# Attention scores with 128 query columns per matmul instead of 64, and values summed in five parts instead of four

## The chip, the cores and the metric

The kernel runs on one core of a Trainium2 chip. The metric is the device time of one execution in microseconds, lower is better. The engines of the core work side by side, each on its own instruction stream: TensorE (PE in the profile; its weight loads are listed apart as PEld), VectorE (DVE), ScalarE (ACT), GpSimd (POOL), and SyncE (SP), whose queue issues nearly all DMA transfers here.

## The reference

Two things follow each other: attention with a bias that depends on relative position, for 8 batches, 8 heads, 576 positions and a head size of 64, and a product of matmuls over all 4608 tokens.

```python
scores = scale * np.matmul(q, k.transpose(0, 1, 3, 2))
pos = np.arange(S)
rel = (pos[:, None] - pos[None, :]).astype(np.float32)
psi_rel = np.log1p(np.abs(rel))
psi_i = np.log1p(np.maximum(pos[:, None].astype(np.float32), 1.0))
x = (psi_rel / psi_i)[..., None]
h = np.maximum(x @ w1 + b1, 0.0)
bias = h @ w2
scores = scores + bias.transpose(2, 0, 1)[None, :, :, :]
scores = scores - np.max(scores, axis=-1, keepdims=True)
attn = np.exp(scores)
attn = attn / (np.sum(attn, axis=-1, keepdims=True) + 1e-09)
return np.matmul(attn, v).astype(np.float32)

a = x @ w1            # x: 4608 x 512, the attention's output
b = x @ w2            # w1, w2: 512 x 1024
h = a * b @ w3        # 1024 x 1024
return (h @ w_out).astype(np.float32)   # 1024 x 512
```

All is float32.

## The kernel before

**Stages.** A prologue (about 52 us) computes the bias table and writes it to DRAM (`bias_group`). Then come 32 attention *units*, one for each pair of heads and batch. Then the weights w3 and w_out are folded into one matrix (`fold`), and the expert stage runs over 9 chunks of 512 tokens (`up`, `down`).

**A unit.** A unit has 2 heads x 576 queries = 1152 query rows, cut into nine score tiles of 128 rows: tiles 0, 2, 4, 6 are the first 512 queries of one head, 1, 3, 5, 7 those of the other, and M holds the last 64 of both. The 576 keys are split in two halves of 288. The key half lies on partitions 0 to 63 or 64 to 127 (head size 64 each), and the queries lie there twice, so both halves of the array's rows can work at once. The steps of a tile t of unit u are:

- `S` (`op_S`, line 254, TensorE): the scores of the tile into a PSUM buffer `s` with two banks, one for each half of the keys. There are two such buffers.
- `T` (`op_T`, line 269, VectorE): scale, add the bias and take the extreme of each row in one instruction, from PSUM into SBUF. It frees the buffer `s`.
- `E` (`op_E`, line 293, ScalarE): the exponential, with the row sums.
- `R` (`op_R`, line 311, VectorE): a transpose in 32 x 32 blocks, for two tiles at a time (M alone), into `PT[u % 2]`.
- `W` (`op_W`, line 348, TensorE): the matmuls of the transposed probabilities with the values into `acc`, over 18 blocks of 32 keys. A unit's 18 blocks are cut by `PARTS` into parts W0, W1, ..., each of which has its own tile of values (`v0`, `v1`, ...; one buffer each), loaded by `lv0`, `lv1`, ... on SP. Each block takes 8 matmuls with 32 rows and 64 columns.
- `X` (`op_X`, ScalarE) copies `acc` to SBUF, and `xd` stores it. There is a single `acc`, so the next unit's W0 waits for X. `r` and `rd` handle the row sums of four units.
- `c0` to `c6` prepare a piece of the expert weights in units that have one (`c0` loads 512 KB).
- `lk`, `lq` load keys and queries.

**Order.** The order on each engine is written out by hand. `rhythm` (line 43) gives each step a time within a period of 12.17 us, and `arrange` shifts it by the unit's number; all steps are then sorted by time and issued, and every engine works strictly in that order. W and its loads lie one period after the scores of the same unit. In the steady state TensorE has this order within a period (the scores of unit u, W0 to W2 of unit u-1, W3 of unit u-2):

```
S0 S2 | W3 | S4 S6 | W0 | SM S1 | W1 | S3 S5 | W2 | S7 (next: S0 S2 ...)
```

VectorE's order is `T0 T2 R57 T4 T6 R02 TM T1 R46 T3 T5 [c5] RM T7 R13`, where R57 and R13 are those of the unit before or of this one, as they come due. With two buffers, S4 needs T0 done, S6 needs T2, SM needs T4, S1 needs T6, S3 needs TM, S5 needs T1, S7 needs T3, S0 of the next unit needs T5, and S2 needs T7.

One float32 matmul of the program appears in the trace as two MATMUL and two LDWEIGHTS records.

Of the kernel before, what the change touches and what calls it, by code (L numbers as in the profile page):

```python
# [18 lines left out]
P = 128  # L19
# [12 lines left out]
FIRST = "02134657M"  # L32
PAIRS = ("02", "46", "M", "13", "57")
NPP, NTS = 2, 3
PARTS = ((0, 5), (5, 9), (9, 12), (12, 18))
T_AT = 0.0, 0.66, 2.63, 3.29, 5.26, 5.92, 7.89, 8.55, 9.91
R_AT = 3.95, 6.58, 9.21, 10.57, PERIOD + 1.32
E_AT = 0.75, 2.75, 3.70, 4.65, 6.25, 7.20, 8.80, 9.75, 10.70
S_AT = -2.32, -1.52, 1.40, 2.00, 4.30, 4.90, 6.90, 7.50, 9.20
W_AT = 2.65, 5.55, 8.15, 11.35  # L40


def rhythm(tiles, turns):

    at = {}
    for n, t in enumerate(tiles):
        at["S" + t] = S_AT[n], "PE"
        at["T" + t] = T_AT[n], "DVE"
# [4 lines left out]
    at["rd"] = PERIOD + 3.80, "SP"  # L53
    for n, w in enumerate(W_AT):
        at[f"W{n}"] = PERIOD + w, "PE"
# [28 lines left out]
def relpos_attention_moe(  # L84
# [25 lines left out]
    HS = S // 2  # L110
# [94 lines left out]
    lo, hi = slice(0, 64), slice(64, 128)  # L205
# [33 lines left out]
    def op_l(u, which):  # L239
        p, b = units[u]  # L240
        n = int(which[1])
        if which[0] == "v":
            b0, b1 = PARTS[n]
            t = vp.tile([P, b1 - b0, 2, D], F32, name=f"v{n}")
# [9 lines left out]
    def op_S(u, t):  # L254

        d = st[u]
        s = d["s", t] = ps_s.tile([P, 2, 512], F32, name="s")
        for hf, rows in enumerate((lo, hi)):
            for g, outs in enumerate((lo, hi)):
                if t == "M":  # L260
                    h, q0 = g, 512
                else:
                    h, q0 = int(t) % 2, int(t) // 2 * P + 64 * g
                nc.tensor.matmul(  # L264
                    s[outs, hf, :HS], d[f"q{h}"][rows, q0:q0 + 64],
                    d[f"k{h}"][rows, :], start=True, stop=True,
                )

# [17 lines left out]
    for i in range(2):  # L286
        t = att.enter_context(tc.tile_pool(name=f"sums{i}", bufs=1)).tile([P, 64], F32, name=f"sums{i}")
# [60 lines left out]
    def op_W(u, n):  # L348
# [4 lines left out]
        acc, pt_ = d["acc"], PT[u % 2]  # L353
        for b in range(*PARTS[int(n)]):
            for a in range(4):
# [37 lines left out]
    def op_c(u, n):  # L393
        pieces[u][int(n)]()

    made = dict(l=op_l, S=op_S, T=op_T, E=op_E, R=op_R, r=op_r, W=op_W, X=op_X, x=op_x, c=op_c)
    later = []
    for (n, u), (at, on) in arrange(NU, pieces).items():
# [14 lines left out]
    with ExitStack() as pro:  # L413
# [29 lines left out]
        def reach(G):  # L443

            return (G + 1) * GR - 1, S - 1 - G * GR
# [9 lines left out]
        for G in range(NGRP):  # L455
            n = max(reach(G)) + 1
# [296 lines left out]
```

## Time and profile before

| | us |
|---|---|
| median of three timed runs | 1150.75 (1145.63 to 1157.9) |
| the profiled execution | 1149.57 |
| its span, first to last instruction | 1147.8 |
| mean granted TensorE clock | 0.985 |

| engine | busy us | share of the span |
|---|---|---|
| TensorE matmuls (PE) | 1070.3 | 93% |
| TensorE weight loads (PEld) | 781.9 | 68% |
| VectorE (DVE) | 638.4 | 56% |
| ScalarE (ACT) | 510.5 | 44% |
| GpSimd (POOL) | 180.2 | 16% |

The page cuts the span into 40 slices of 28.7 us and gives a digit of busy tenths for each. The granted clock is the share of its full speed that TensorE was allowed. Groups of instructions are named by line, engine, operation and tile (`out<-in`), with count, busy time, mean duration, and the idle time before them with what ended it ("issue": nothing that the profile shows). Matmuls are pipelined and the ends that the trace gives them are modelled, so from one burst of matmuls to the next it is the distance of starts that counts.

### The profile page before, as it was taken

What the parts mean: (1) busy time and instruction counts of PE and PEld (TensorE: products, weight loads), DVE (VectorE), ACT (ScalarE), POOL (GpSimd) and SP (SyncE); (2) the same over time, 40 slices, a digit from 0 to 9 for tenths busy, and PEclk for the clock granted to TensorE, in tenths of its full rate; (3) what the DMA queues carried; (4) which work ended last, traced back from release to release, by engine and by line L of the source; (5) the groups of instructions that cost most, each with busy time, mean ns of one, the idle gap of its engine ahead of it and who ended that gap; (6) DMA issues with size and microseconds to landing.
All of it is one profiled execution on the core that took longest, in us unless ns stands there. A gap on an engine that the chain in (4) does not pass through costs nothing.

```text
span 1147.8 us, 34051 instructions
## 1 busy us (share of the span) xinstructions
PE 1070.3 (93%) x14720; PEld 781.9 (68%) x14720; DVE 638.4 (56%) x1204; ACT 510.5 (44%) x1111; POOL 180.2 (16%) x167
## 2 busy tenths in 40 slices
PE   7888888888888999898999999999999999999998
PEld 2245555555555655576888888888888888888887
DVE  8997989889988999956551313222231322223111
ACT  7876767676766778765442111111212112121212
POOL 0022312230323033254350000000000000000000
PEclk9988999999989999999999999999999999999999
DMA  8966757767777667456240202111121202110000
GB/s 275 319 194 217 253 178 256 243 197 225 240 245 227 214 209 244 140 167 174 83 120 37 58 16 76 35 58 53 40 70 37 56 19 74 37 37 1 37 1 37
DMA packets 95957, 149.16 MB, mean 130 GB/s; under 512 B 22336, under 2 KB 49088, under 8 KB 95808
## 3 DMA queue, kind: packets, MB, share of 16 engines
q1 hardware_dynamic: 95376, 146.98, 40.4%
q8 instruction: 115, 1.88, 0.7%
q14 instruction: 34, 0.28, 0.1%
q10 hardware_dynamic: 432, 0.02, 0.0%
HBM read 116.93 MB, written 30.03 MB: 128 GB/s over the span
## 4 chain that ended last, share of the span: by engine, by line
PE 72%; DVE 13%; issue 8%; ACT 3%; DMA 2%; POOL 1%; SPq 1%; DVEq 0%; ACTq 0%; POOLq 0%
PE up L623 34%; PE o L648 17%; PE acc L360 9%; PE s L264 7%; DVE ts L275 6%; DVE pt L314 5%; PE bacc L485 3%; ACT x L369 1%; PE wacc L582 1%; DMA x_d<-x 1%; DMA v<-in_v_dram 0%; DVE wmag L159 0%; DMA rb<-r_m 0%; DVE mx L275 0%; ACT x L374 0%
## 5 line engine op out<-in xcount | busy, mean ns | idle before, releaser
L304 ACT ACTIVATE pp<-ts,mx 128x576 f32<-128x576 f32 x256 | 197.1, 770 | 103.4 <-DVE mx L275 102.4
L631 DVE TENSOR_TENSOR g<-up,a 128x512 f32<-128x512 f32 x72 | 49.8, 691 | 343.7 <-PE up L623 343.7
L360 PE MATMUL acc<-pt,v 32*64 32x128 f32 (+1 forms) x9216 | 208.1, 299 | 34.2 <-issue 27.9
L360 PEld LDWEIGHTS acc<-pt,v 32*64 32x64 f32 x9216 | 163.9, 133 | 99.2 <-issue 72.8
L623 PE MATMUL up<-xh,wl 128*128 128x512 f32 x576 | 225.1, 391 | 0.0
L623 PE MATMUL up<-xl,wh 128*128 128x512 f32 x576 | 225.1, 391 | 0.0
L623 PE MATMUL up<-xh,wh 128*128 128x512 f32 x576 | 225.1, 391 | 0.0
L264 PE MATMUL s<-k,q 64*64 64x288 f32 x2304 | 190.1, 434 | 25.0 <-DVE mx L275 24.2
L275 DVE CUSTOM_DVE_ANT_0 ts<-s,nb 128x576 f32<-128x576 f32 x256 | 183.4, 741 | 38.2 <-PE s L264 38.1
L648 PE MATMUL o<-w3s,gh 128*128 128x512 f32 x576 | 177.7, 390 | 0.0
L314 DVE STREAM_TRANSPOSE pt<-pp 128x1152 f32<-128x1152 f32 x128 | 175.9, 1375 | 0.0
L628 ACT COPY a<-up 128x512 f32<-128x512 f32 x72 | 42.2, 587 | 263.0 <-PE up L623 263.0
L264 PEld LDWEIGHTS s<-k,q 64*64 64x64 f32 x2304 | 74.5, 136 | 104.2 <-DVE mx L275 64.1
L623 PEld LDWEIGHTS up<-xl,wh 128*128 128x128 f32 x576 | 108.2, 188 | 23.4
L623 PEld LDWEIGHTS up<-xh,wl 128*128 128x128 f32 x576 | 108.2, 188 | 23.4
L623 PEld LDWEIGHTS up<-xh,wh 128*128 128x128 f32 x576 | 108.2, 188 | 23.4
L648 PEld LDWEIGHTS o<-w3s,gh 128*128 128x128 f32 x576 | 108.1, 188 | 22.9
L634 ACT ACTIVATE gh<-g 128x512 fp32r<-128x512 f32 x72 | 45.5, 632 | 173.7 <-DVE g L631 173.7
L648 PE MATMUL o<-w3s,gl 128*128 128x512 f32 x288 | 112.1, 389 | 0.0
L609 POOL TENSOR_SCALAR xh<-xr 128x512 fp32r<-128x512 f32 x36 | 22.6, 627 | 447.0 <-DVE xr L605 446.0
L155 POOL TENSOR_SCALAR wmag<-wmag 128x512 f32<-128x512 f32 x24 | 46.0, 1917 | 245.8 <-ACT wmag L145 245.8
L637 DVE TENSOR_TENSOR gl<-g,gh 128x512 fp32r<-128x512 f32 x72 | 50.8, 705 | 51.3 <-ACT gh L634 51.2
(68 smaller groups left out, 902.8 us busy)
## 6 DMA issues: line engine op xcount, KB each, us to landing
q<-in_q_dram SPq DMA_DIRECT2D x64, 288.0 KB, 4.0
wi<-in_moe_w_dram SPq DMA_DIRECT2D x32, 512.0 KB, 4.7
v<-in_v_dram SPq DMA_DIRECT2D x32, 384.0 KB, 5.4
nb_d<-bev SPq DMA_DIRECT2D x36, 295.5 KB, 4.7
v<-in_v_dram SPq DMA_DIRECT2D x32, 320.0 KB, 4.1
k<-in_k_dram SPq DMA_DIRECT2D x64, 144.0 KB, 3.4
nb<-nb_d SPq DMA_DIRECT2D x16, 576.0 KB, 5.8
x_d<-x SPq DMA_DIRECT2D x32, 288.0 KB, 4.8
```

What stands on the lines that cost most here:

```text
L155: clamps.tensor_scalar(d["mag"], d["mag"], LEAST, MOST, op0=ALU.max, op1=ALU.min)
L264: nc.tensor.matmul(s[outs, hf, :HS], d[f"q{h}"][rows, q0:q0 + 64], d[f"k{h}"][rows, :], start=True, stop=True,)
L275: nc.vector.tensor_tensor_reduce(out=halves(ts), in0=d.pop(("s", t))[:, :, :HS], in1=halves(NB[p, t]), op0=ALU.add, op1=ALU.min, scale=-1. ...
L304: nc.scalar.activation(d["p", ps][:, k * S:(k + 1) * S], ts, AF.Exp, bias=mx, scale=-1.0, accum_out=SUMS[u // 4 % 2][:, col:col + 1],)
L314: nc.vector.transpose(o, st[u].pop(("p", ts)))
L360: nc.tensor.matmul(acc[outs, a, c0:c0 + 32 * (t1 - t0)], d["v", b][rows, h], pt_[rows, t0:t1, 32 * b:32 * b + 32], start=(b == 0), stop=(b ...
L623: nc.tensor.matmul(acc, l[:, cc], r, start=(n == 0), stop=(n == 3 * NC - 1))
L628: nc.scalar.copy(a, ps[0])
L631: nc.vector.tensor_tensor(g, ps[1], a, op=ALU.mult)
L634: nc.scalar.activation(gh, g, AF.Copy)
L637: nc.vector.tensor_tensor(gl, g, f(gh), op=ALU.subtract)
L648: nc.tensor.matmul(d["o", t], l[:, sl], folded[ft][:, r], start=(ft == 0 and n == 0), stop=(ft == NF - 1 and n == 2),)
```

## The change

Tiles 0 to 7 of the scores are computed by two matmuls (one per half of the keys) that take all 128 queries as columns, instead of four that take 64 each. Tile M, whose two halves belong to different heads, keeps its four. The 18 blocks of values are cut into five parts (4, 4, 3, 4 and 3 blocks) instead of four (5, 4, 3 and 6), each with its own tile of values and its own load, and the times of the score and value steps in the period are moved. On TensorE the order becomes

```
S0 | W3 | S2 | W4 | S4 S6 | W0 | SM S1 | W1 | S3 S5 | W2 | S7 (next: S0 ...)
```

with W3 and W4 those of unit u-2. VectorE's and ScalarE's orders stay as they are. On SP there is one more load of values in a unit, `lv4`.

```diff
-PARTS = ((0, 5), (5, 9), (9, 12), (12, 18))
+PARTS = ((0, 4), (4, 8), (8, 11), (11, 15), (15, 18))
...
-S_AT = -2.32, -1.52, 1.40, 2.00, 4.30, 4.90, 6.90, 7.50, 9.20
-W_AT = 2.65, 5.55, 8.15, 11.35
+S_AT = -2.40, -0.55, 1.40, 2.00, 4.30, 4.90, 6.90, 7.50, 9.00
+W_AT = 2.65, 5.55, 7.95, 10.20, 12.25
...
         for hf, rows in enumerate((lo, hi)):
-            for g, outs in enumerate((lo, hi)):
-                if t == "M":
-                    h, q0 = g, 512
-                else:
-                    h, q0 = int(t) % 2, int(t) // 2 * P + 64 * g
+            if t == "M":
+                parts = [(outs, g, 512, 64) for g, outs in enumerate((lo, hi))]
+            else:
+                parts = [(slice(0, P), int(t) % 2, int(t) // 2 * P, P)]
+            for outs, h, q0, n in parts:
                 nc.tensor.matmul(
-                    s[outs, hf, :HS], d[f"q{h}"][rows, q0:q0 + 64],
+                    s[outs, hf, :HS], d[f"q{h}"][rows, q0:q0 + n],
                     d[f"k{h}"][rows, :], start=True, stop=True,
                 )
```

## The prediction

> **What bounds the kernel now.** I read the page first, then busy time by stretches, then the waits, then the order of one clean unit of work and of one disturbed one.
>
> ```profile
> span 1147.8 us, 34051 instructions
> PE 1070.3 (93%) x14720; PEld 781.9 (68%) x14720; DVE 638.4 (56%) x1204; ACT 510.5 (44%) x1111; POOL 180.2 (16%) x167
> DVE  8997989889988999956551313222231322223111
> q8 instruction: 115, 1.88, 0.7%
> PE 72%; DVE 13%; issue 8%; ACT 3%; DMA 2%; POOL 1%; SPq 1%; DVEq 0%; ACTq 0%; POOLq 0%
> ```
>
> VectorE is dense for the first 17 slices of 28.7 us (attention) and thin after them (the expert matmuls, where TensorE is dense). The change touches attention alone. The profiled execution took 1149.57 us, 1.8 us more than its span and 1.2 us under the median of the three timed runs (1150.75 us); I work against 1149.6.
>
> Two stretches follow: all of attention, and one unit (a head pair of one batch) inside it.
>
> ```profile
> 288.60:300.80 12.20, 11.08 (x378) 7.06 (x364) 12.20 (x25) 9.74 (x24) 3.19 (x2) 1.00 0.69 212
> 52.00:486.00 434.00, 376.36 (x11215) 232.90 (x11211) 394.47 (x780) 306.73 (x738) 108.23 (x87) 0.96 0.69 220
> ```
>
> After the length come PE, PEld, DVE, ACT, POOL with instruction counts, then granted clock, DMA share and GB/s. In the clean unit VectorE never rests (12.20 of 12.20), and TensorE has 1.12 us free. So VectorE sets the pace, nothing in the change shortens its work, and only its idle time can be won: 434.00 - 394.47 = 39.5 us in the whole of attention. The waits say for whom:
>
> ```profile
> PEld s L264 <- DVE mx L275: 64.1, 113, 2.0
> DVE ts L275 <- PE s L264: 40.7, 36, 4.1
> PE acc L360 <- issue: 27.9, 18, 3.3
> PEld acc L360 <- ACT x L374: 18.2, 29, 0.7
> ```
>
> Line 2: VectorE waits 40.7 us, 36 times, for score tiles. Line 3: TensorE, in the middle of the value matmuls, stands still 18 times for nothing that a semaphore shows, 27.9 us. One such case, TensorE, VectorE and the DMA engines around it:
>
> ```profile
> 197.14 0.79 PE L360 MATMUL acc<-pt,v 32*64 32x160 f32 x30
> 201.06 0.70 PE L360 MATMUL acc<-pt,v 32*64 32x160 f32 x18 [3.14 <-issue]
> ...
> 204.57 2.59 PE L360 MATMUL acc<-pt,v 32*64 32x160 f32 x96
> ...
> 202.58 0.76 DVE L275 CUSTOM_DVE_ANT_0 ts<-s,nb 128x576 f32<-128x576 f32 x1 [2.99 <-PE s L264]
> ...
> 196.00:198.00 2.00, 1.92 (x51) 1.00 (x47) 2.00 (x4) 1.57 (x6) 0.94 (x1) 1.00 0.97 338
> 198.00:200.00 2.00, 0.00 (x0) 0.00 (x0) 1.59 (x4) 1.56 (x4) 0.94 (x1) 1.00 1.05 395
> 204.00:206.00 2.00, 2.00 (x59) 1.43 (x55) 2.00 (x6) 1.42 (x4) 1.05 (x1) 0.50 0.73 207
> ```
>
> After 30 of 48 matmuls of W2 TensorE pauses 3.14 us; the DMA engines are full (0.97, 1.05) just then; VectorE pays 2.99 us; and the clock granted afterwards is 0.50, so that 96 matmuls take 2.59 us. The page's queue of instructions carried 115 packets, 1.88 MB: 16.3 KB each, and 2 x 14720 / 115 = 256 TensorE instructions each. I read these pauses as **instruction blocks that come late through busy DMA engines**. This is inferred from the coincidence, not shown.
>
> **The order in a clean unit**, from which the changed order is priced (start, modelled duration, idle before):
>
> ```profile
> 287.49 0.72 PE L264 MATMUL s<-k,q 64*64 64x288 f32 x8 [0.63 <-DVE mx L275]
> 288.13 1.91 PE L360 MATMUL acc<-pt,v 32*64 32x160 f32 x96
> 289.97 1.20 PE L264 MATMUL s<-k,q 64*64 64x288 f32 x16
> 291.35 1.67 PE L360 MATMUL acc<-pt,v 32*64 32x160 f32 x80 [0.18 <-ACT x L374]
> 292.94 1.20 PE L264 MATMUL s<-k,q 64*64 64x288 f32 x16
> 294.07 1.37 PE L360 MATMUL acc<-pt,v 32*64 32x160 f32 x64
> 295.37 1.20 PE L264 MATMUL s<-k,q 64*64 64x288 f32 x16
> 296.50 1.09 PE L360 MATMUL acc<-pt,v 32*64 32x160 f32 x48
> 297.53 1.20 PE L264 MATMUL s<-k,q 64*64 64x288 f32 x16
> 299.67 0.72 PE L264 MATMUL s<-k,q 64*64 64x288 f32 x8 [0.95 <-DVE mx L275]
> ...
> 288.64 0.72 DVE L275 CUSTOM_DVE_ANT_0 ts<-s,nb 128x576 f32<-128x576 f32 x1
> 291.27 0.72 DVE L275 CUSTOM_DVE_ANT_0 ts<-s,nb 128x576 f32<-128x576 f32 x1
> 293.89 0.72 DVE L275 CUSTOM_DVE_ANT_0 ts<-s,nbM 128x576 f32<-128x576 f32 x1
> 300.83 0.72 DVE L275 CUSTOM_DVE_ANT_0 ts<-s,nb 128x576 f32<-128x576 f32 x1
> ```
>
> A burst of two score tiles (16 records) lasts 1.13 us from its start to the next start (292.94 to 294.07), a lone tile 0.64 (287.49 to 288.13): a tile streams in 0.49 us, and a burst adds 0.15. Value matmuls: 96 in 1.84 us, 48 in 1.03 (296.50 to 297.53): 16.9 ns each and 0.22 per burst. One more burst of each kind in a unit therefore costs 0.37 us of TensorE.
>
> **The change, part by part.**
>
> *Two wide score matmuls for four narrow ones.*
>
> ```profile
> L264 PE MATMUL s<-k,q x2304: 399/403/739, 51.3 to 484.3; 64*64 64x288 f32 x192
> L264 PEld LDWEIGHTS s<-k,q x2304: 129/133/228, 51.3 to 484.0; 64*64 64x64 f32 x192
> L623 PEld LDWEIGHTS up<-xh,wh 128*128 128x128 f32 x576 | 108.2, 188 | 23.4
> ```
>
> Eight records of 403 ns fit into 0.49 us, so now the two halves of the keys and the two halves of the queries run side by side. With 128 query columns two matmuls lie side by side and stream the same 288 keys: I take 0.49 us again. No row shows this form. From below nothing can be gained in streaming, since the same keys pass; from above, if the two did not overlap, a tile costs 0.98. A weight load of 128 columns takes 188 ns (the expert matmuls' row) against 133: **+55 ns**. Inside a burst it hides behind the previous pass (0.24 us, half a tile); at the start of each of five bursts it doesn't: +0.27 us a unit. Records of L264 fall from 2304 to 2 x 32 x (8 x 2 + 4) = 1280 of each kind (M keeps four matmuls a tile), so attention issues 2 x 11213 - 2048 = 20378 TensorE instructions where it issued 22426: **9% less, 8 blocks of 256 fewer**.
>
> *Five value parts of 4, 4, 3, 4, 3 key blocks for 5, 4, 3, 6.* The order on TensorE goes from `S7 S0 S2 | W3 | S4 S6 | W0 | ...` to `S7 S0 | W3 | S2 | W4 | S4 S6 | W0 | ...`: matmuls in all unchanged, one score burst and one value burst more, +0.37 us a unit. Since M keeps its narrow form, the array also changes form between SM and S1; I price this as one more burst's fixed part, +0.15. In the clean unit S2 waits behind T7 with 0.95 us of idle, and W3 queues behind it. Now 64 value matmuls (1.30 us) run in that hole: S0 ends near 298.7, W3 near 300.0, S2 near 300.7; its reader T2 follows T0 (300.83 + 0.72), so S2 has 0.8 us to spare. W4 (48, 1.03 us) ends near 301.75; S4's buffer is free when T0 is done (301.55). Before, W3 ended at 302.16 on the same scale. So S4 comes 0.4 us sooner, against 0.05 for its wider load. W0 still waits for X (line 291.35), but with 64 matmuls ends 0.27 us sooner. The tightest place now is SM: it starts at 292.94, is done 0.64 later at 293.58, and TM starts at 293.89, **0.31 us of slack**; it becomes 0.31 + 0.27 = **0.58** (SM itself stays narrow; S1 behind it ended at 294.07, is due when TM is done, 294.61, and gains 0.27 less 0.15 and 0.05).
>
> *TensorE's account.* +0.37 + 0.27 + 0.15 = +0.79 us a unit, covered by the 1.12 us of idle; 0.33 is left. Without cover it would cost 32 x 0.79 = 25 us.
>
> *Loads.* The v parts change size with the blocks, bytes alike; 32 more issues on SP's queue. SP holds 1% of the chain; lv3 is issued when W3 has read its tile, ahead of c0 and xd, and W3 now ends sooner, so I cost it at nothing. If W3 were late, c0, xd and rd would queue behind that wait, but their readers come microseconds later. X follows W4 instead of the long W3, and ScalarE takes it behind E0 either way: nothing. The sums at the end (last units, expert stage) keep their work: nothing, within 1 us.
>
> **The Trainium skill** (Runtime: NRT & Kernel Launch, Instruction fetch mechanics) also says that instructions come in 16 KiB blocks of 256 while the previous block runs, and that crossing a boundary is "mostly hidden". The 16.3 KB per packet agrees; the 3.14 us pause does not look hidden. By that sentence fewer instructions win nothing, and the sum would be that of the second rival below.
>
> **The sum.** 18 pauses cost VectorE 40.7 us, 2.26 each (the 27.9 is only the part in which the array's modelled matmuls had ended). 9% fewer blocks: 1.6 fewer pauses, -3.7 us. The 16.4 that stay: a unit has (9 x 4 + 18 x 8) x 2 x 2 = 720 TensorE instructions and will have 656, so a block of 256 lasted 12.2 x 256 / 720 = 4.34 us and will last 4.76. A late block is late by up to 0.42 us less (0 if it is asked for only just before it is needed); I take 0.33, since most of a block's time, not all, should lie between request and need. Slack at the tightest place adds 0.27 (0 if a pause falls elsewhere); I take 0.22. 16.4 x 0.55 = -9.0 us. Together -12.7: 1149.6 - 12.7 = **1136.9**, say 1137; with both at nothing it is 1146, with both in full 1134.6.
>
> **Rivals.**
>
> 1. *The pauses belong to the transfers* (no difference). For: DMA share 0.97 and 1.05 at the pause shown; a block that is microseconds late because of 0.5 MB loads is not helped by 0.33. Against: most pauses are shorter than 3.3 us (27.9 / 18 = 1.55), where 0.55 is a third. Then only the 8 blocks count: -3.7, 1146. The three runs before already differ by 12 us, as chance arrival would make them.
>
> 2. *Nothing is hidden and nothing won* (slower): TensorE takes the lead from VectorE. Mechanism: the array changes from full-width score tiles to quarter-height value tiles eleven times a unit (SM to S1 counted) instead of eight. It decides from +1.12 us a unit; I count +0.79, so 0.03 us more per change is enough, and from there each 0.1 us per change costs 32 x 1.1 = 35 us. Taking the whole 0.79 uncovered: 1149.6 + 25 = 1175. For: SM's slack and the wait for X leave small holes, not one large one. Against: 0.33 is left, and 0.15 per score burst already holds both changes. The Trainium skill (TensorEngine Tiling, Key Properties) says that changing the tiling mode drains TensorE; the 0.15 and 0.22 agree, and no row here shows it for full width.
>
> 3. *The pauses nearly vanish*: if the missing lead is what turns late blocks into pauses, lead and slack take three quarters: 1149.6 - 30 = 1119. For: 18 pauses in 88 blocks, so the others just arrive. Against: the 3.14 us case.
>
> 4. *Wide matmuls don't overlap* (the change doesn't do what it says): 8 x 0.49 = 3.9 us a unit; TensorE 11.08 + 0.79 + 3.9 = 15.8 against 12.2; 32 x 3.6 = +115, 1265.
>
> **How the numbers follow.** Forecast 0.50 (own range 1127 to 1144), first rival 0.24, second 0.13, third 0.10, fourth 0.03. The range leaves out the fourth, the upper half of the second and the lowest part of the third: 1117 to 1162. One per cent, about what a measurement of this kernel can tell from no change, is 11.5 us. Under 1138 to 1139 lie 0.8 of the forecast and the third, 0.50; same has the rest of the forecast and the first, 0.34; slower the second and fourth, 0.16.
>
> **What would show it.** Score records 1280, a tile still 0.49 us apart in a burst (0.98: rival 4). First pass after a switch longer by about 55 ns. VectorE's wait for scores down from 40.7 to some 28 us, pauses in the value matmuls 16 or fewer; unchanged pauses mean rival 1. S2's idle before it gone from the clean unit, and a clean unit still 12.2 us; if VectorE waits in units without a pause, rival 2 is right. Wrong altogether would be a VectorE instruction that grew, or an expert stage that moved by more than 2 us.

## The result and the profile after

The changed kernel takes 1145.23 us (median of 21 runs, 1135.57 to 1148.85), the kernel before 1154.62 us in its 21 runs (1144.84 to 1163.95). The ratio is **0.9922, with a 95% interval of 0.9898 to 0.9946**: 9 us less, under one per cent. The forecast was 12.7 us less. A single run of either kernel scatters over 13 to 19 us, so differences of medians under some 4 us say little below. Sets of runs taken at different times differ too: the same changed kernel stands at 0.9879 and at 0.9839 [0.9799, 0.9879] of the kernel before in the two later sets. Kernels are therefore compared with those measured beside them.

The profiled execution took 1142.65 us. Its page, the parts that answer to those of before (length and counts; the instruction queue; TensorE's score matmuls by shape, from the groups with shapes kept apart):

```profile
span 1140.9 us, 32065 instructions
PE 1086.7 (95%) x13696; PEld 801.6 (70%) x13696; DVE 637.3 (56%) x1204; ACT 510.2 (45%) x1111; POOL 179.9 (16%) x167
q8 instruction: 107, 1.75, 0.6%
L264 PE MATMUL s<-k,q 64*128 64x288 f32 x1024 | 178.3, 453 | 9.0 <-DVE mx L275 3.7 <-DVE pt L314 2.5 <-issue 1.9
L264 PEld LDWEIGHTS s<-k,q 64*128 64x128 f32 x1024 | 86.6, 192 | 71.4 <-DVE mx L275 31.4 <-issue 27.2 <-DVE pt L314 3.7
```

TensorE has 2 x 1024 instructions less, and 8 packets fewer came over the instruction queue (107 for 115): 2 x 13696 / 107 is 256 again. The waits of attention, as before from 52 to 486 us (total, times, longest):

```profile
PEld s L264 <- DVE mx L275: 35.6, 106, 2.3
DVE ts L275 <- PE s L264: 28.0, 27, 2.5
PEld acc L360 <- ACT x L374: 20.6, 30, 1.2
PE acc L360 <- issue: 19.5, 15, 2.7
```

VectorE's wait for scores fell from 40.7 to 28.0 us, the pauses of TensorE in the value matmuls from 18 to 15. A clean unit (first the whole unit, then TensorE in order of time, then three of VectorE's reads):

```profile
289.10:301.30 12.20, 11.72 (x336) 7.57 (x335) 12.20 (x25) 10.05 (x25) 4.52 (x4) 1.00 0.83 281
...
291.82 1.40 PE L360 MATMUL acc<-pt,v 32*64 32x160 f32 x64 [0.48 <-ACT x L374]
293.14 1.40 PE L264 MATMUL s<-k,q 64*64 64x288 f32 x12
294.48 1.37 PE L360 MATMUL acc<-pt,v 32*64 32x160 f32 x64
...
297.97 1.24 PE L264 MATMUL s<-k,q 64*128 64x288 f32 x8
299.14 1.47 PE L360 MATMUL acc<-pt,v 32*64 32x160 f32 x64
300.54 0.76 PE L264 MATMUL s<-k,q 64*128 64x288 f32 x4
301.22 1.06 PE L360 MATMUL acc<-pt,v 32*64 32x160 f32 x47
...
294.37 0.71 DVE L275 CUSTOM_DVE_ANT_0 ts<-s,nbM 128x576 f32<-128x576 f32 x1
301.30 0.71 DVE L275 CUSTOM_DVE_ANT_0 ts<-s,nb 128x576 f32<-128x576 f32 x1
301.95 0.75 DVE L275 CUSTOM_DVE_ANT_0 ts<-s,nb 128x576 f32<-128x576 f32 x1
```

VectorE still fills the unit, 12.20 us as before, so nothing was won in this unit, which has no pause. Two wide tiles last 1.17 us (297.97 to 299.14) for 1.13, a lone one 0.68 for 0.64; S2 starts with no idle before it.

**Where the rest stayed.** Attention ends 12.8 us sooner (VectorE's last read of scores ends at 472.9 us for 485.7), but the first matmul of the expert stage starts only 6.9 us sooner (545.9 for 552.8). The stretch between grew from 67.1 to 73.0 us; the expert stage behind it takes 595.0 us in both. TensorE in that stretch, and the granted clock with the DMA share (last three columns: clock, share, GB/s):

```profile
474.19 0.66 PE L570 MATMUL w3t<-ident,w3s 128*128 128x128 f32 x4
475.84 1.88 PE L360 MATMUL acc<-pt,v 32*64 32x160 f32 x93 [0.99 <-ACT x L374]
480.45 1.86 PE L360 MATMUL acc<-pt,v 32*64 32x128 f32 x35 [2.74 <-issue]
482.25 0.80 PE L582 MATMUL wacc<-woh,w3h 128*128 128x512 f32 x1
482.84 0.63 PE L582 MATMUL wacc<-wol,w3h 128*128 128x512 f32 x1
483.27 0.63 PE L582 MATMUL wacc<-woh,w3l 128*128 128x512 f32 x1
...
478.00:480.00 2.00, 0.00 (x0) 0.00 (x0) 1.31 (x3) 2.00 (x5) 0.71 (x1) 1.00 0.14 24
482.00:484.00 2.00, 2.00 (x6) 1.47 (x5) 0.33 (x1) 0.00 (x0) 1.48 (x1) 0.50 0.03 8
484.00:486.00 2.00, 2.00 (x6) 1.52 (x6) 0.00 (x0) 0.00 (x0) 0.00 (x0) 0.50 0.67 221
...
q8 instruction: 1, 0.02, 2.2%
```

A pause of 2.74 us stands in the value matmuls of the last unit, and the folding matmuls behind it run at clock 0.50, 0.43 us apart where they are 0.23 apart at full clock. The last line is the DMA queues' answer for 477.4 to 480.5 us: one block of instructions came over the queue within the pause. In the kernel before, the same run of value matmuls goes through in one piece:

```profile
488.66 2.73 PE L360 MATMUL acc<-pt,v 32*64 32x160 f32 x144 [1.56 <-ACT x L374]
```

The end of a block lay there before the change too. The change takes away 2 x 1024 instructions, exactly 8 blocks of 256, so the ends of the later blocks hardly move against the program: counted through the traces, a block ends behind the 91st matmul of that run before the change and behind the 93rd after it. What differs is when the next block comes. Before, TensorE enters the block ahead of it at 485.67 us and the packet with the next one starts at 486.46, 0.8 us later. After, it enters at 473.46 and the packet starts at 477.95, 4.5 us later. Both times SyncE issues two loads of 512 KB of expert weights close to the entry, 0.07 us behind it before the change, 0.54 us ahead of it after. Below are those issues, before and after, and the DMA engines after the change, in 40 slices of 0.3 us from 470 to 482 us (they are full from 474.5 to 477.5):

```profile
485.74 0.93 SPq L140 DMA_DIRECT2D wi<-in_moe_w_dram  x2
472.92 0.93 SPq L140 DMA_DIRECT2D wi<-in_moe_w_dram  x2
DMA  9487000597100679999999999740241002989961
```

### The profile page after: what moved, and what is told of

Its sections match the earlier page's. It is cut to its first block, busy times and chain, and to the rows that moved or that the text cites. A ratio compares the mean times of both kernels' runs of the same rounds, so it can differ in the third digit from the quotient of the medians.

```text
span 1140.9 us, 32065 instructions
## 1 busy us (share of the span) xinstructions
PE 1086.7 (95%) x13696; PEld 801.6 (70%) x13696; DVE 637.3 (56%) x1204; ACT 510.2 (45%) x1111; POOL 179.9 (16%) x167
## 3 DMA queue, kind: packets, MB, share of 16 engines
q1 hardware_dynamic: 99984, 146.98, 40.7%
## 4 chain that ended last, share of the span: by engine, by line
PE 71%; DVE 16%; issue 7%; DMA 2%; ACT 2%; SPq 1%; POOL 0%; DVEq 0%; ACTq 0%; POOLq 0%
PE up L623 35%; PE o L648 17%; PE acc L360 8%; DVE pt L314 7%; PE s L264 7%; DVE ts L275 6%; PE bacc L485 3%; PE wacc L582 1%; DVE zdve L471 1%; ACT x L369 1%; DVE mx L275 1%; DMA nb<-nb_d 0%; DMA rb<-r_m 0%; DVE wmag L159 0%; DMA x_d<-x 0%
## 5 line engine op out<-in xcount | busy, mean ns | idle before, releaser
L360 PE MATMUL acc<-pt,v 32*64 32x128 f32 (+1 forms) x9216 | 214.7, 299 | 27.1 <-issue 19.5
L264 PE MATMUL s<-k,q 64*128 64x288 f32 (+1 forms) x1280 | 200.0, 450 | 10.6 <-DVE mx L275 4.9
L264 PEld LDWEIGHTS s<-k,q 64*128 64x128 f32 (+1 forms) x1280 | 93.9, 180 | 81.0 <-DVE mx L275 35.6
```

Source lines behind the costliest of these rows:

```text
L264: nc.tensor.matmul(s[outs, hf, :HS], d[f"q{h}"][rows, q0:q0 + n], d[f"k{h}"][rows, :], start=True, stop=True,)
L360: nc.tensor.matmul(acc[outs, a, c0:c0 + 32 * (t1 - t0)], d["v", b][rows, h], pt_[rows, t0:t1, 32 * b:32 * b + 32], start=(b == 0), stop=(b ...
```

## The experiments

The theory (A) is the prediction's: a pause of TensorE is a block of 256 instructions that comes late through busy DMA engines; the wide form wins by fewer instructions, the five parts by slack. The main rival (B): the order of the parts wins everything.

**One half of the change each.** The wide matmuls with the old parts and times:

```diff
-PARTS = ((0, 4), (4, 8), (8, 11), (11, 15), (15, 18))
+PARTS = ((0, 5), (5, 9), (9, 12), (12, 18))
-S_AT = -2.40, -0.55, 1.40, 2.00, 4.30, 4.90, 6.90, 7.50, 9.00
-W_AT = 2.65, 5.55, 7.95, 10.20, 12.25
+S_AT = -2.32, -1.52, 1.40, 2.00, 4.30, 4.90, 6.90, 7.50, 9.20
+W_AT = 2.65, 5.55, 8.15, 11.35
```

> Only the wide score matmuls; four value parts and the step times as before. If the gain comes from instruction blocks that are fewer and less late (theory A, the prediction's): pauses in the value matmuls at 15 or 16 for 18, and about 9 us less than before (the -3.7 for fewer blocks and 16.4 x 0.33 = -5.4 for lead). If it comes from the order of the parts (theory B): no gain, or up to 8 us slower, because the first load of each burst is 55 ns longer (four bursts, 0.2 us a unit) and S2's wait for T7 still stands in front of W3.

Measured: 1146.35 us against 1153.93 for the kernel before, measured beside it, ratio 0.994 [0.9911, 0.9969]: 7 us less. Its profile has 12 pauses in the value matmuls, 18.1 us together, where 15 or 16 were expected, and VectorE waits 33.6 us for scores. And the new parts and times with the four narrow matmuls, an edit of the kernel before:

```diff
-PARTS = ((0, 5), (5, 9), (9, 12), (12, 18))
+PARTS = ((0, 4), (4, 8), (8, 11), (11, 15), (15, 18))
-S_AT = -2.32, -1.52, 1.40, 2.00, 4.30, 4.90, 6.90, 7.50, 9.20
-W_AT = 2.65, 5.55, 8.15, 11.35
+S_AT = -2.40, -0.55, 1.40, 2.00, 4.30, 4.90, 6.90, 7.50, 9.00
+W_AT = 2.65, 5.55, 7.95, 10.20, 12.25
```

> Only the five value parts and the new step times; four narrow score matmuls a tile as before. Theory A: the same number of instructions, so 17 to 18 pauses; only the slack gains, 18 x 0.22 = about 4 us less than before. Theory B (order): the whole 9 us or more.

Measured: 1146.5 us, 0.9933 [0.9902, 0.9964]: 7 to 8 us less. Its profile has 18 pauses in the value matmuls, as expected, but VectorE waits 39.4 us, hardly less than 40.7; that execution took 1153.98 us, 7.5 us over the median, so it shows little of the gain. So neither half has it all, and B falls as a whole: the wide form, at the old order, gains. But the shares were mis-sized (9 and 4 expected, 7 and 7 to 8 measured), and together they give 9, not 15. The intervals are each some 7 us wide, so a sum of 12 isn't excluded. The late block in the last value matmuls doesn't explain the missing rest, since the five parts alone have it too (2.06 us, at 493.95); the rest stays open.

**The loads taken away.** Both kernels without the loads of values after the first unit:

```diff
         if which[0] == "v":
             b0, b1 = PARTS[n]
+            if u > 0:
+                for i in range(b0, b1):
+                    st[u]["v", i] = st[0]["v", i]
+                return
```

> The kernel before, without the loads of values after the first unit (all units use the first unit's values): 36 MB less read during attention, everything else alike. If the pauses are instruction blocks that come late through busy DMA engines: at most 5 pauses of over 0.5 us are left, VectorE's wait for scores falls from 40.7 to under 10 us, and the time by about 30 us. If the pauses have another cause on TensorE: 15 or more pauses stay, and the time falls by under 8 us.

> The changed kernel, without the loads of values after the first unit. If the whole gain of the change lies in pauses and in VectorE's waits behind them: within 0.3% of the kernel before with the same loads left out. If the change also shortens the units without a pause: still some 5 to 9 us faster than that kernel. If its extra 0.79 us of TensorE a unit costs time where no pause hides it: slower than that kernel.

Measured: before without loads 1124.73 us (0.9749 [0.9713, 0.9785]: 29 us less), after without loads 1115.81 us (0.9665 [0.9629, 0.9701]). VectorE's waits, the pauses in the value matmuls, and the stretch from 52 to 486 us with the DMA share (last but one column), first the kernel before, then the changed one:

```profile
DVE ts L279 <- PE s L268: 17.0, 16, 3.6
PE acc L364 <- issue: 9.8, 9, 2.8
52.00:486.00 434.00, 384.90 (x11596) 241.41 (x11589) 407.01 (x803) 323.95 (x774) 120.79 (x97) 0.98 0.46 144
```

```profile
DVE ts L279 <- PE s L268: 7.7, 10, 2.4
PE acc L364 <- issue: 6.5, 6, 2.6
52.00:486.00 434.00, 408.77 (x10622) 267.96 (x10621) 411.72 (x813) 327.65 (x780) 124.50 (x100) 0.99 0.48 150
```

The kernel before falls by 29 us, its DMA share in attention from 0.69 to 0.46, its pauses from 18 (27.9 us) to 9 (9.8 us), and its VectorE waits 17.0 us for 40.7: busy DMA engines are behind the larger part of the pauses. I had expected under 10 us of wait and at most 5 pauses of over 0.5 us; 6 of that length are left for 16, so the values' loads are not the only ones in the way. Between the two light kernels the change still gains 8.9 us, as much as with loads. That was noted as the mark of units that get shorter without a pause, but it need not be: VectorE's wait accounts for it, 17.0 - 7.7 = 9.3 us. The pauses that remain are fewer with the change (6 for 9) and cost VectorE less.

**The instruction count put back.** The changed kernel with each wide matmul cut in two by keys: the same shape and columns, 8 records a tile as before the change.

```diff
+        cuts = ((0, HS),) if t == "M" else ((0, HS // 2), (HS // 2, HS))
+        for c, e in cuts:
...
-                    s[outs, hf, :HS], d[f"q{h}"][rows, q0:q0 + n],
-                    d[f"k{h}"][rows, :], start=True, stop=True,
+                        s[outs, hf, c:e], d[f"q{h}"][rows, q0:q0 + n],
+                        d[f"k{h}"][rows, c:e], start=True, stop=True,
```

> The changed kernel, with each wide score matmul cut in two by keys (144 each): as many TensorE instructions as before the change (8 records a tile), the same shape and the same columns streamed. If the number of instructions is what the wide form wins (theory A): the wide form's part of the gain goes, back to the kernel with the five parts alone, about 2 to 7 us slower than the changed kernel, with a tile still 0.49 us. If the count doesn't matter: within 1 us of the changed kernel. If the 128-column loads can't hide behind a pass of 0.12 us, a tile takes more than 0.6 us and the time rises by over 10 us; then it tells nothing of the count.

Measured: 1149.32 us, 0.9951 [0.9915, 0.9988], against 0.9879 [0.9832, 0.9927] for the changed kernel measured beside it. Two tiles in a unit of its profile, and its waits in attention:

```profile
294.39 1.25 PE L266 MATMUL s<-k,q 64*128 64x144 f32 x16
295.57 1.10 PE L362 MATMUL acc<-pt,v 32*64 32x160 f32 x48
...
DVE ts L277 <- PE s L266: 26.8, 27, 2.0
PE acc L362 <- issue: 22.9, 19, 3.0
```

Two tiles take 1.18 us (1.17 uncut), so the cut costs TensorE nothing by itself, and yet the median is 4 us above the changed kernel's 21 runs, 10 above those measured beside it. The trace has 14720 matmul records again, and TensorE pauses 19 times in the value matmuls for 14 in the changed kernel. So the number of instructions seems to count, but this is the weakest of the results: the two intervals overlap at their ends, and the profile doesn't show the cost. VectorE waits 26.8 us in it, no more than in the changed kernel, in an execution of 1141.77 us, 7.6 us under the median.

**The changed kernel again**, to see how far one profile carries:

> The changed kernel once more, beside the three others of this call, to see how far a single profile can be trusted: about 9 us less than before; pauses and VectorE's wait for scores within a fifth of 17 and 28.0 us if they are a property of the program, far from them if the arrival of instruction blocks is chance.

Measured: 1139.18 us, 0.9879 [0.9832, 0.9927]; in its profile VectorE waits 27.9 us for scores, and TensorE pauses 14 times in the value matmuls. With a third profile below (30.7 us, 17 times) the wait repeats within a tenth, and many of the pauses stand at the same instruction, though not all.

**The order alone.** S2 back in front of W3:

```diff
-S_AT = -2.40, -0.55, 1.40, 2.00, 4.30, 4.90, 6.90, 7.50, 9.00
+S_AT = -2.40, -2.10, 1.40, 2.00, 4.30, 4.90, 6.90, 7.50, 9.00
```

> The changed kernel with S2 put back in front of W3 (order S7 S0 S2, W3, W4): the four bursts of before, wide matmuls, parts of 4, 4, 3 and 7 blocks in effect. If the hole in front of S2 is what the order wins: S2's wait for T7 is back in every unit (VectorE's side unchanged in units without a pause) and the time is 3 to 7 us above the changed kernel. If W0's shorter part (SM's slack) is what the order wins: within 2 us of the changed kernel.

Measured: 1142.83 us, 0.9897 [0.9854, 0.9941]: 3.6 us above the changed kernel measured beside it, not separable by these runs. Its profile:

```profile
PEld s L264 <- DVE mx L275: 63.1, 123, 2.7
DVE ts L275 <- PE s L264: 34.9, 29, 3.8
```

The wait in front of S2 is back (63.1 us for 38.2 in the changed kernel measured beside it), and VectorE waits 7 us more; but the stretch after the last T is 67.3 us for 70.7, so half comes back there: the same block ends behind the 93rd matmul of the last run, but its packet starts 0.6 us after TensorE enters the block ahead, and there is no pause. The hole is worth something in attention; in the time it isn't shown.

And S2 behind the whole of W3, wide, with the four parts of before:

```diff
-PARTS = ((0, 4), (4, 8), (8, 11), (11, 15), (15, 18))
-S_AT = -2.40, -0.55, 1.40, 2.00, 4.30, 4.90, 6.90, 7.50, 9.00
-W_AT = 2.65, 5.55, 7.95, 10.20, 12.25
+PARTS = ((0, 5), (5, 9), (9, 12), (12, 18))
+S_AT = -2.40, 0.50, 1.40, 2.00, 4.30, 4.90, 6.90, 7.50, 9.00
+W_AT = 2.65, 5.55, 7.95, 10.80
```

> Wide matmuls, the four parts of before (5, 4, 3, 6 blocks), but S2 behind W3 (order S7 S0, W3, S2 S4 S6, W0): fills the hole in front of S2 without a fifth burst, 0.37 us of TensorE a unit less than the changed kernel; but S2 is done only 0.3 us before T2 is due, and SM has its old slack of 0.31 us. If TensorE's free time is what counts: 2 to 5 us faster than the changed kernel. If slack at the tightest place counts: 3 to 8 us slower than it, near the kernel before.

Measured: 1163.2 us, 1.0074 [1.0043, 1.0105]: slower than before the change, by more than I had put on it. It has a burst less of TensorE work than the changed kernel, S2 no longer waits in front of W3, and it is the slowest of all.

```profile
DVE ts L275 <- PE s L264: 49.8, 54, 3.9
PE acc L360 <- issue: 23.1, 19, 3.4
```

VectorE waits 54 times where TensorE pauses 19 times: with S2, S4 and S6 in a row behind six blocks of values, score tiles are late without any pause in that place. At 282.48 us, for example, T2 waits 0.30 us for S2, some 15 us after the last pause of over 0.4 us. So free time of TensorE is not what counts here. I read it as **how long before its need each tile is done**; the slack itself was not varied alone in this run.

**Slack, and the block's end.** Two changes to the changed kernel. First, the ends of instruction blocks moved by 144 instructions, with one small matmul in each of 36 groups of the prologue (this moves them in attention as well):

```diff
             acc = psb.tile([P, 1024], F32, name="bacc")
+            nc.tensor.matmul(acc[0:GM, 0:16], w2b, zs[0][:, 0:16], start=True, stop=True)
```

> The changed kernel with one small matmul more in each of the 36 bias groups of the prologue (16 columns, written over by the matmul that follows): 144 more TensorE instructions long before attention, nothing else. In both profiles of the changed kernel TensorE pauses 2.7 us in the last value matmuls, and the clock is 0.50 for 5 us after. If pauses come at the ends of blocks of 256 instructions, the block's end moves by 144 instructions out of these value matmuls into slow weight-folding matmuls: the pause and the half clock there are gone, the stretch from the last T to the first matmul of the expert stage is 4 to 5 us shorter (67 to 68 for 71 to 73), and the time is 3 to 5 us less than the changed kernel's. If the pause belongs to the place in the program (the weight loads, the switch of stages): it stays, and the time is the same or up to 1 us longer.

Second, one block of values moved from W0 to W4:

```diff
-PARTS = ((0, 4), (4, 8), (8, 11), (11, 15), (15, 18))
+PARTS = ((0, 3), (3, 7), (7, 10), (10, 14), (14, 18))
```

> The changed kernel with parts of 3, 4, 3, 4 and 4 key blocks (for 4, 4, 3, 4, 3): one block moved from W0 to W4, where S4 had 1.1 us of slack. The tightest slack of a score tile rises from 0.58 us (SM, S3) to about 0.7 (S2). If slack at the tightest place decides what a pause costs VectorE: 2 to 4 us less than the changed kernel. If not: the same within 1 us.

Both together, and the changed kernel as their reference (the kernel before took 1160.22 us beside these, some 6 us more than in the other sets):

> shift and p34344 together: 5 to 9 us less than the changed kernel if both readings hold; 3 to 5 if only the block's end counts.

> The changed kernel as the reference of this call: 9 to 14 us less than before, the pause of 2.7 to 3.0 us in the last value matmuls once more.

| kernel | median us | ratio to before | VectorE waits for scores, us | last T to first expert matmul, us |
|---|---|---|---|---|
| changed (after_third) | 1144.07 | 0.9839 [0.9799, 0.9879] | 30.7 | 71.2 |
| block's end moved (shift) | 1136.08 | 0.9781 [0.9736, 0.9825] | 27.5 | 68.1 |
| 3, 4, 3, 4, 4 (p34344) | 1137.25 | 0.9790 [0.9748, 0.9833] | 24.0 | 69.1 |
| both | **1132.47** | **0.9751 [0.9715, 0.9786]** | 18.3 | 67.8 |

The last value matmuls, first in the changed kernel measured beside them, then with the block's end moved:

```profile
479.66 1.88 PE L360 MATMUL acc<-pt,v 32*64 32x160 f32 x93 [0.71 <-ACT x L374]
484.29 1.03 PE L360 MATMUL acc<-pt,v 32*64 32x128 f32 x35 [2.75 <-issue]
```

```profile
478.34 2.45 PE L360 MATMUL acc<-pt,v 32*64 32x160 f32 x128 [1.28 <-ACT x L374]
480.72 0.50 PE L583 MATMUL wacc<-woh,w3h 128*128 128x512 f32 x1
481.06 0.40 PE L583 MATMUL wacc<-wol,w3h 128*128 128x512 f32 x1
481.29 0.40 PE L583 MATMUL wacc<-woh,w3l 128*128 128x512 f32 x1
```

In all three profiles of the changed kernel the pause stands in the same run of 128 matmuls, behind the 93rd (475.84, 479.66 and, in the other one, 476.40). Shift the count by 144 and all 128 run in one piece, with the folding matmuls at full clock behind them. A pause is tied to a place in the count of instructions, not to a place in the program. The stretch is 3.1 us shorter (4 to 5 expected); the rest of the 8 us is not explained by it (3 to 5 expected in all). VectorE's wait is 3 us lower too, and the interval is wide. Moving one block of values gains 7 us where 2 to 4 were expected, with 4 to 7 us less wait than in the changed kernel's profiles, although its pause in the last value matmuls stays (2.79 us). Both together gain 11.6 us, more than the 5 to 9 expected, and make the fastest kernel here that loads all values.

**Where the pauses stand.** The traces show what the pauses are. Count TensorE's matmuls, weight loads and semaphore instructions from the start of a trace up to each pause of over 0.4 us that the profile puts down to "issue". Divided by 256, the count leaves 192 or 193 for every one of them, 220 pauses in 14 profiles: they stand only where one block of 256 meets the next. The packets of the instruction queue say why only some ends pause. In the changed kernel, between 75 and 500 us, the next block's packet started less than 2 us after TensorE entered the block ahead at 48 block ends, and at none of them TensorE paused in this way; it started later at 32, and at 15 of them TensorE paused. In these 15 TensorE went on 2.2 to 2.7 us after the packet's start.

## Why the prediction was right or wrong

- *What bounds, and what could be won.* Right. VectorE's instructions and the clean unit (12.20 us) did not change; VectorE's wait fell from 40.7 to 28.0 us, where 28 had been named (27.9 and 30.7 in the two other profiles; the kernel before has one).
- *0.49 us a wide tile.* Right: 1.17 - 0.68 = 0.49. The load's +55 ns at a burst's start shows as +0.04 (1.13 to 1.17, 0.64 to 0.68). SM and S1 together last 1.34 us (293.14 to 294.48), 0.21 more than before; 0.20 had been put on the change of form and the load. The fourth rival is out.
- *The account and the slack.* TensorE's busy time in the clean unit went from 11.08 to 11.72 us, +0.64 for the +0.79 priced. SM is done at 293.14 + 0.64 = 293.78 and TM starts at 294.37: 0.59 us of slack, 0.58 predicted. S2 ends at 301.22, 0.73 before T2 (301.95); 0.8 predicted. The second rival is out in this kernel; in the variant with S2 behind the whole W3, which has less TensorE work, late tiles did make it slower than before. The danger was in the slack, not in the account.
- *Pauses are late blocks.* Only inferred in the prediction; now it is shown, by the 29 us less without the values' loads, the shift of the pause with the count, and the place of all 220 pauses at block ends. The lead that the prediction assumed is borne out too: with the way free, a block's packet starts soon after TensorE enters the block ahead (0.6 to 0.8 us in the cases below). The first rival (transfers decide alone, 1146) names the cause rightly, and its time is nearer to the measured 1145.2 than mine. But it would leave VectorE's wait near 37 us, and it is 28.0; and by the gain, 9.4 us measured, its 3.7 is further off than 12.7.
- *The sum.* Its total for attention came out in this pair of profiles (12.7 us of wait gone, 12.8 us sooner done). That is in part luck, since its two parts did not: the wide form alone gains 7 us where 9 stood, the parts 7 to 8 where 4 stood, and moving one block, for some 0.12 us more slack by the expectation, gained 7 us where 2 to 4 were expected. The term *slack, 0.22 us a pause* looks too small. That sum counted one place and one wait a pause; how a pause spreads over several tiles wasn't priced, and no run isolates it.
- *The base.* The sum starts from one profiled execution of the kernel before, 1149.6 us; its median over 21 runs is 1154.6. So of the 8.3 us between 1136.9 and 1145.2, 5.0 lie in the base and 3.3 in the gain (12.7 named, 9.4 measured).
- *The step that failed* is "the sums at the end keep their work: nothing, within 1 us". The work there did stay, but the stretch between attention and the expert stage grew by 73.0 - 67.1 = 5.9 us (by 3.6 and 4.1 in the two other profiles), so that much of the 12.7 us won in attention was given back. What the runs show in its place is a late block: 2.74 us of pause in the last run of value matmuls and 2.1 us at half clock (the 12 folding matmuls behind it take 4.99 us, and 2.89 where the block's end is moved away). It is not the smaller number of instructions that brought it, since 8 whole blocks less hardly move the later ends, and the two kernels with the five parts and the full number pause there as well (2.06 us, and 3.00 with the cut matmuls). The block's packet starts 0.6 to 0.8 us after TensorE enters the block ahead in four kernels that don't pause there (the kernel before, the wide form alone, S2 in front of W3, S2 behind W3). It starts 4.1 to 4.6 us after it in those that do. There the 1 MB of weights is issued 0.2 to 0.8 us ahead of the entry, in the four from 0.3 ahead of it to 0.1 behind. That the new order's timing against this load makes the block late is read from these traces; no run moved the load, so this last cause stays open.
- *One reading.* From "fewer instructions win nothing" the prediction goes to its second rival, 1175. That doesn't follow: the slack term would be left, 18 x 0.22 = 4 us, and the sum near 1146.

The chances: faster by over 1% had 0.50; the ratio of 0.9922 falls to the 0.34 of no difference by that bound. The time lies within the range, which is wide enough to hold the kernel before as well (1154.6), and just above the forecast's own range of 1127 to 1144.

## What to carry to other kernels

When one engine runs tens of instructions in a microsecond, count its instructions as a resource: here blocks of 256 came through the same DMA engines as the data, and a late one stopped the engine for up to 3.4 us. An edit can bring or remove a late block in a stage that it doesn't touch, by its timing or, as the 144 instructions did here, by moving the blocks' ends, so look for pauses there, and try a shift of the count before judging it. With an engine at its limit, what a neighbour's pause costs depended here on how early each of its results was ready: order the neighbour's work by the slack of the tightest result, not by its idle time.

## What the runs showed of the hardware

A row-half matmul with 128 columns in float32 ran beside one on the other half at almost no loss: two tiles of 288 keys took 1.17 us, for 1.13 as quarter-array matmuls. TensorE's pauses stood at the ends of blocks of 256 instructions, 220 of 220, and ended 2.2 to 2.7 us after the late block's packet started (15 pauses of the changed kernel). After a pause the granted clock was often 0.50, for 3.4 or 6.8 us at a time: 3.4 us from 485.2 in the third profile of the changed kernel, behind a pause of 2.75 us, and 6.8 us from 480.1 in the first, behind one of 2.74. By my estimate that costs up to half of this time on top of the pause. It isn't always so: in the kernel with parts of 3, 4, 3, 4 and 4 the folding matmuls behind a pause of 2.79 us start 0.24 us apart, as at full clock.
